# A fused state-space mixer with an MLP gate: four weight loads on another queue, two exponentials on another engine, another order

## The chip, the cores and the metric

The kernel runs on one core of a Trainium2 chip. The core has four compute engines that run side by side, each with its own instruction stream: TensorE (PE in the profile) multiplies matrices into PSUM, VectorE (DVE) and ScalarE (ACT) work on SBUF and PSUM, GpSimd (POOL) works on SBUF. SyncE (SP) issues transfers; ScalarE and GpSimd have queues for transfers too. Engines wait for each other through semaphores. The metric is the time of one execution in microseconds, here the median of several runs.

## The reference, cut to what matters

```python
xn = layernorm(x)                                 # x: 1 x 2048 x 448
dt = exp(log_dt); Lam_bar = exp(dt * Lam)         # Lam complex, 448 states
B_bar = ((Lam_bar - 1) / Lam)[:, None] * Bmat
Bu = einsum("bld,pd->blp", xn, B_bar)
h[t] = Lam_bar * h[t-1] + Bu[t]                   # over 2048 steps
s = 2 * Re(einsum("blp,dp->bld", h, Cmat)) + xn * Dskip
m = gelu(layernorm(xn) @ w1 + b1) @ w2 + b2       # 448 -> 1792 -> 448
out = x + s * silu(m)
```

Inputs and output are bfloat16.

## The kernel before, in words

The 2048 positions are cut into 8 blocks of 256, a block into its even and its odd positions (par 0 and 1), each 128 rows on the partitions. Two blocks make a group of 512 positions; the loop over the four groups is written out by `STEPS`. For each group:

- VectorE takes the statistics (bn_stats, L399; for group 0's first layer norm L431), makes the factors (`ln_scale`), and VectorE or ScalarE apply them (L499, L500). A DMA transpose or TensorE turns the normalized rows into columns.
- `mm1_run` (L801) multiplies by w1. The contraction over 448 goes in halves of 64 rows, two at a time on two halves of TensorE. ScalarE applies GELU out of PSUM (L805). `mm2` (L828) multiplies by w2; VectorE adds the bias (L831); ScalarE makes SiLU (L833) or tanh (L835).
- `bu` (L729) multiplies by the input matrix BT; the result u is copied out of PSUM (`copy`, L417). `ssm` turns u by tables of sines and cosines WT (L744 to L748), scans along the positions with the decay dk (L753, L755), copies the scanned states to bf16 (L417), and turns them back (L771 to L775). L773 and L775 write the state h_sb; L775, called hh below, is the part for the last 64 states.
- `ym` (L871, L877) multiplies the state by CZ (even positions, with M applied to xn, L874) or CQ (odd positions). VectorE multiplies by the gate (L885, L888) and adds x (L891), and the result is written out.

Before that, tables are made: the parameter columns in `parameters` (three vectors of 448 turned into columns by TensorE at L529, then dozens of operations on 128 x 4 at L534 to L566), a range reduction `wrap` and a sine polynomial, the tables WT and dk in `tables`, the matrices CZ, CQ and BT's second half with `combine` (a scaled tmp at L658 or L659, and a multiply-add at L661), and M in `m0`.

Group 0's first two blocks have a start of their own. `first_stats` takes statistics and makes the layer norm factor 1/sqrt(var'). For block 0 ScalarE does it for each parity by Ln and Exp (L434, L435), for block 1 for both parities at once (L438, L439). `first_apply` applies the factor on VectorE (L453), TensorE transposes (L460) and L417 copies the result out of PSUM. `dummies` (L422) are matmuls of ones that fill TensorE's time ahead of the work. ScalarE's function tables have to be loaded: Ln and Exp at the start (L314), GELU in `gelu_table` (L443), Sin and SiLU (L614), GELU again (L618).

w1 lies in SBUF as 128 rows x 4 x 1792. `ldw1` loads it in four pieces of columns; for each piece one transfer brings rows 0 to 383 and a second one the last 64 rows (w1r), both on SyncE's queue; the low half of the last slice is copied on the chip (L352). `ldx` loads x by blocks; the one of blocks 2 and 3 is SyncE's twelfth transfer.

The order of the work is not found at run time. The builder functions only list tasks, each with what it reads and writes. `Plan.emit` then issues them in the order of `ORDER`, a list of task numbers written out by hand; each engine's instruction stream is that list filtered to its tasks. Where a task can run on one of two engines (`small`: GpSimd or VectorE; `copy`: ScalarE or VectorE; `combine`, `ln_apply`, output adds), it goes to the second one if its number stands in `SECOND`. Waits on semaphores are put in from the reads and writes.

## Time and profile before

| what | value |
|---|---|
| median of three runs | 153.37 us (153.15 to 153.41) |
| span of the profiled execution | 151.8 us |
| TensorE busy | 147.1 us, 97% |
| VectorE busy | 127.6 us, 84% |
| ScalarE busy | 99.0 us, 65% |
| GpSimd busy | 42.1 us, 28% |

The span goes from the first to the last instruction of the profiled execution; what a run's time has beside it lies around it. A row of the timeline has the start and the duration in us, the engine, the line of the kernel, the operation, the tiles, and in brackets the idle time ahead of it and what ended that; rows of like instructions are drawn together (x8). In the chain that ended last each piece is a start, a duration and what ran. The groups of instructions have busy time and the mean of one in ns. Matmuls overlap in their pipeline, so the mean duration of one is longer than the step from one start to the next.

```profile
PE   7899999999999999999999999999999999999992
...
DVE  2874999999978979999999996379968726999984
ACT  3888996988789559997898610463579834067400
POOL 5376827153020920010456006200072031000201
PEclk9999999999999999999999999999999999999999
DMA  4999999989997300700003032610331001100022
```

These rows of the page cut the span into 40 slices; a digit is the busy share in tenths.

### The profile page before, as it was taken

The page shows a single profiled execution, that of the slowest core. Times are in us where ns is not written, and L with a number is a line of the kernel's source. Part 1 is how long each engine was busy: PE and PEld are TensorE (multiplying, and loading weights), DVE is VectorE, ACT ScalarE, POOL GpSimd, SP SyncE. Part 2 cuts the span into 40 slices and gives each one's busy share as a digit, 9 for nine tenths or more (in the row PEclk, how much of TensorE's full clock was granted, in tenths as well). Part 3 has the DMA queues.
Part 4 walks back from the last instruction along what each step waited for, and adds up shares of the span by engine and source line. Part 5 has one row for each costly group of instructions (what it writes and reads, how often), then busy time and mean ns, then how long its engine had stood idle before and what let it go on. Part 6 is the DMA issues. An engine that isn't in the chain of part 4 may idle for free.

```text
span 151.8 us, 2974 instructions
## 1 busy us (share of the span) xinstructions
PE 147.1 (97%) x1127; PEld 86.6 (57%) x1127; DVE 127.6 (84%) x267; ACT 99.0 (65%) x183; POOL 42.1 (28%) x101
## 2 busy tenths in 40 slices
PE   7899999999999999999999999999999999999992
PEld 7785755454566577545444556764454666555551
DVE  2874999999978979999999996379968726999984
ACT  3888996988789559997898610463579834067400
POOL 5376827153020920010456006200072031000201
PEclk9999999999999999999999999999999999999999
DMA  4999999989997300700003032610331001100022
GB/s 116 262 305 390 266 202 138 219 152 133 165 261 180 65 0 0 138 0 4 0 0 63 4 60 45 154 60 4 60 101 23 0 4 57 64 0 0 4 84 98
DMA packets 31236, 14.73 MB, mean 97 GB/s; under 512 B 24752, under 2 KB 30774, under 8 KB 31222
## 3 DMA queue, kind: packets, MB, share of 16 engines
q1 hardware_dynamic: 30912, 14.26, 41.8%
q0 software_dynamic: 160, 0.23, 1.0%
q8 instruction: 9, 0.15, 0.4%
q10 hardware_dynamic: 150, 0.05, 0.1%
q14 instruction: 5, 0.04, 0.1%
HBM read 6.89 MB, written 1.84 MB: 57 GB/s over the span
## 4 chain that ended last, share of the span: by engine, by line
PE 80%; DVE 9%; DMA 4%; SPq 4%; issue 2%
PE psum L828 23%; PE psum L801 22%; PE psum L729 14%; PE psum L871 13%; DMA x_all<-in_A_x_dram 4%; PE psum L874 4%; SPq L84 4%; PE psum L712 3%; DVE xn_sb L499 2%; DVE lnst L399 1%; DVE s_w L628 1%; PE psum L877 1%; DVE o L831 1%; PE psum L697 1%; DVE tmp L891 1%
## 5 line engine op out<-in xcount | busy, mean ns | idle before, releaser
L801 PE MATMUL psum<-xn2T,w_sb 64*128 64x512 bf16 (+1 forms) x462 | 44.6, 345 | 0.3 <-ACT xn2T L417 0.2
L828 PE MATMUL psum<-w_sb,gT 128*128 128x448 bf16 x224 | 44.5, 353 | 0.2 <-DVE o L831 0.2
L805 ACT ACTIVATE gT<-psum,b1f 128x512 bf16<-128x512 f32 (+1 forms) x66 | 35.9, 625 | 10.4 <-PE psum L801 10.2
L801 PEld LDWEIGHTS psum<-xn2T,w_sb 64*128 64x128 bf16 x462 | 24.1, 109 | 19.8 <-ACT gT L805 2.3
L828 PEld LDWEIGHTS psum<-w_sb,gT 128*128 128x128 bf16 x224 | 21.5, 98 | 20.7 <-DVE o L831 0.6
L417 ACT ACTIVATE u_sb<-psum 128x512 bf16<-128x512 f32 (+2 forms) x22 | 10.5, 478 | 23.0 <-PE psum L729 22.7
L729 PE MATMUL psum<-xnT,BT 128*128 128x256 bf16 x196 | 24.0, 273 | 0.0
L729 PEld LDWEIGHTS psum<-xnT,BT 128*128 128x128 bf16 x196 | 18.9, 98 | 5.4 <-issue 1.1
L891 POOL TENSOR_TENSOR tmp<-t,x_all 128x448 bf16<-128x448 bf16 x5 | 5.2, 1032 | 33.1 <-DVE t L888 30.7
L753 DVE TENSOR_TENSOR_SCAN s_w<-dk,vs 128x774 f32<-128x774 f32 x8 | 14.0, 1760 | 0.1
L500 ACT ACTIVATE xn_sb<-x_all,lnw 128x448 bf16<-128x448 bf16 (+2 forms) x21 | 13.0, 662 | 1.2 <-DVE xn_sb L499 1.1
L417 ACT ACTIVATE vs<-s_w 64x256 bf16<-64x256 f32 (+2 forms) x16 | 10.9, 681 | 2.6 <-DVE s_w L753 1.5
L871 PE MATMUL psum<-CZ,h_sb 128*128 128x448 bf16 x56 | 11.9, 352 | 0.0
L871 PE MATMUL psum<-CQ,h_sb 128*128 128x448 bf16 (+2 forms) x54 | 10.5, 332 | 0.0
L399 DVE BATCH_NORM_STATS2 lnst<-x_all 128x6 f32<-128x448 bf16 x12 | 7.1, 617 | 3.4 <-DMA x_all<-in_A_x_dram 3.4
L831 DVE TENSOR_TENSOR o<-psum,b2bc 128x448 f32<-128x448 f32 x16 | 9.7, 614 | 0.2
L871 PEld LDWEIGHTS psum<-CZ,h_sb 128*128 128x128 bf16 x56 | 5.4, 98 | 4.7 <-DVE lnmv L405 0.4
L871 PEld LDWEIGHTS psum<-CQ,h_sb 128*128 128x128 bf16 x54 | 5.1, 98 | 4.0 <-DVE t L885 0.4
L874 PE MATMUL psum<-M,xnT 128*128 128x448 bf16 x32 | 7.4, 352 | 0.0
L480 POOL TENSOR_TENSOR lnw<-lnw,mhalf 128x8 f32<-128x8 f32 x3 | 7.2, 2404 | 0.3
L883 DVE TENSOR_TENSOR Cr<-psum,xd 128x448 f32<-128x448 f32 x7 | 4.3, 620 | 3.5 <-PE psum L877 3.4
L499 DVE TENSOR_SCALAR xn_sb<-x_all,lnw 128x448 bf16<-128x448 bf16 (+2 forms) x19 | 6.9, 396 | 0.0
(160 smaller groups left out, 189.1 us busy)
## 6 DMA issues: line engine op xcount, KB each, us to landing
out_dram<-tmp SPq DMA_DIRECT2D x7, 224.0 KB, 2.0
x_all<-in_A_x_dram SPq DMA_DIRECT2D x3, 448.0 KB, 4.0
w_sb<-in_B_w_dram SPq DMA_DIRECT2D x3, 448.0 KB, 8.4
w_sb<-in_B_w_dram SPq DMA_DIRECT2D x3, 384.0 KB, 4.8
vs<-in_A_C_re_dram SPq DMA_DIRECT2D x1, 392.0 KB, 11.6
Bn<-in_A_B_im_dram SPq DMA_DIRECT2D x1, 336.0 KB, 10.2
Bn<-in_A_B_re_dram SPq DMA_DIRECT2D x1, 336.0 KB, 10.5
vs<-in_A_C_im_dram SPq DMA_DIRECT2D x1, 336.0 KB, 10.8
```

The source lines that it names most:

```text
L399: dve([lambda e, b=b, par=par, q=q: e.bn_stats(lnst[:, q, :], x_all[:, 2 * g + b, par, :])], [f"x{2 * g + b}"] , [f"st{q}"], 0.62, prio)
L417: kb.either(("act", [lambda e, o=o, i=i: e.activation(o, i, ACT.Copy) for o, i in pairs]), ("dve", [lambda e, o=o, i=i: e.tensor_copy(o, i ...
L499: on = [("dve", [lambda e, o=o, i=i: e.tensor_scalar(o, i, rs, nb, op0=ALU.mult, op1=ALU.add) for o, i in parts], 0.4, 0.12), ("act", [lam ...
L500: ("act", [lambda e, o=o, i=i: e.activation(o, i, ACT.Identity, bias=nb, scale=rs) for o, i in parts], 0.75, 0.2)]
L729: fns = [lambda e, r=r, m=m, d=d: e.matmul(psum[:, 4, r * NK:(r + 1) * NK], BT[:, m, d, :], xnT[:, gx, d, :], start=(d == 0), stop=(d == 6 ...
L753: dve(lambda e, so=so, vi=vi: e.tensor_tensor_scan(so, dk[:].rearrange("p i c -> p (i c)"), vi, 0.0, ALU.mult, ALU.add), ["v", "vl", "dk", ...
L801: return lambda e: e.matmul(view(bk[k]), w1_sb[rows, d, fcol(2 * j + k)], rhs[rows, d, :, :], start=not second and n == 0, stop=second and ...
L805: act([lambda e, k=k: e.activation(gT[:, gb, 2 * j + k, :].rearrange("p (r c) -> p r c", r=2)[:, :, cols], view(bk[k]), ACT.Gelu_apprx_tan ...
L828: fns = [lambda e, fi=fi: e.matmul(psum[:, bk, 0:D], gT[:, gb, fi, q * 128:(q + 1) * 128], w2_sb[:, fi, :], start=(fi == 0), stop=(fi == N ...
L831: dve(lambda e: e.tensor_tensor(o2[:, fb, :], psum[:, bk, 0:D], b2bc[:], ALU.add), [f"ps{bk}", "b2bc"], [f"oo{fb}"], 0.62, prio - 76)
L871: fns = [lambda e, k=k: e.matmul(psum[:, bk, c0:c1], h_sb[:, hb, k, k0:k0 + 128], cm[:, k, c0:c1], start=(k == 0), stop=False) for k in ra ...
L874: fns += [lambda e, d=d: e.matmul(psum[:, bk, c0:c1], xnT[:, gx, d, xs], M0[:, d, c0:c1], start=False, stop=(d == 3)) for d in range(4)]
```

## The change

Four things change.

1. The four transfers of w1's last 64 rows are issued by ScalarE instead of SyncE.
2. Block 1's two layer norm factors are no longer made by Ln and Exp on ScalarE. A `small` task w11 computes var' (VectorE in the new lists), and GpSimd raises it to the power -1/2 (128 x 2). The decay R1 = exp(A1) is no longer an Exp on ScalarE; GpSimd raises a constant e, set by a new memset, to the power A1 (128 x 4).
3. The task that loads the GELU table reads only dt and block 0's factors, no longer R1 and block 1's factors.
4. `ORDER` and `SECOND` are new throughout. By task numbers, the list has two more tasks (the memset and w11), so numbers from 14 on are shifted by one or two against the old list.

What the new lists say for the start: ScalarE issues Lambda_im, log_dt, w1r of piece 1, Lambda_re, then loads the first table, makes a factor of block 0, issues w1r of piece 0, makes the other factor, and issues w1r of pieces 2 and 3 around its copy of the second transposed half; the first half's copy is VectorE's. SyncE's order is the two halves of x block 0, block 1, w1 pieces 1, 0, 2, 3, then x blocks 2 and 3 as the eighth transfer, then w2. TensorE's eight dummies stand ahead of the parameter matmuls. Further on, fifteen of the parameter operations, the wrap, carries and some output adds go from GpSimd to VectorE; a dozen copies, tmp halves and layer norm applies go from ScalarE to VectorE, and about as many from VectorE to ScalarE, among them the |.| of the tables. The last column of CZ is computed after group 0's state instead of before it.

```diff
 ORDER = [int(k) for k in """
-0 13 19 47 9 16 18 20 14 1 94 26 17 95 91 27 92 21 15 24 48 4 96 12 108 93 90 109 97 104 103 25 105 99 22 98 49 50 55 5 51 65 106 2 110 100 111 107 29
-101 112 30 56 28 52 114 23 54 32 53 131 57 117 128 31 118 113 121 170 115 33 46 132 168 133 129 39 130 34 66 171 253 250 102 119 155 40 123 251 252
...
+48 17 9 20 25 19 18 28 21 2 3 16 12 27 14 13 4 15 0 26 22 95 6 30 1 96 92 97 33 91 23 93 110 47 49 100 94 111 105 50 31 40 106 52 98 5 51 107 41 112
+108 53 113 109 42 54 34 114 99 116 101 43 29 104 171 115 39 102 172 120 103 24 119 38 117 121 67 133 130 206 123 170 118 157 134 32 131 173 124 125
...
+617 622 627 624 631 628 625 629 632 626 633 630 634
 """.split()]
 SECOND = [int(k) for k in """
-45 53 54 61 63 66 69 74 76 83 112 130 133 158 160 162 163 165 177 184 185 187 189 190 220 222 224 226 228 230 238 248 249 258 266 268 331 362 364 365
-384 400 401 436 447 468 480 482 487 491 499 501 502 504 510 528 529 609 612 627
+46 55 59 62 63 64 68 70 71 72 73 74 76 77 78 81 82 83 84 85 86 88 102 109 114 132 135 160 163 164 167 186 189 190 191 196 198 204 222 226 230 232 234
+246 248 250 251 260 270 326 355 356 364 366 399 403 404 405 452 470 482 503 504 506 507 509 510 514 518 527 530 532 533 576 591 614 629
 """.split()]
...
 
         ident = SB("ident", [128, 128])
         mhalf = SB("mhalf", [128, 1, 1], F32)
+        euler = SB("euler", [128, 1], F32)
         dk = SB("dk", [128, 3, NK + 2], F32)
         iota = dk[:, 0, 0:NK]
         sgn = SB("sgn", [128, 4], F32)
...
             pool(lambda e: e.memset(M0[:, 3, :], 0.0), [], ["M0p"], 0.3, S0 + 1)
             pool(lambda e: e.memset(h_sb[:, :, :, 0:2], 0.0), [], ["hp0", "hp1"], 0.2, S0 + 1)
             pool(lambda e: e.memset(mhalf[:], -0.5), [], ["mhalf"], 0.1, S0 + 1)
+            pool(lambda e: e.memset(euler[:], math.e), [], ["euler"])
             pool(lambda e: e.memset(eps[:, 0:1], LN_EPS), [], ["eps"], 0.1, S0)
             pool(lambda e: e.memset(eps[:, 1:2], LN_EPS * LN_EPS), ["eps"], ["eps"], 0.1, S0)
 
...
             def ldw1(cs, prio):
                 a, w = CH[cs[0]][0] * 128, sum(CH[c][1] for c in cs) * 128
                 ld("sp", w1_sb[:, 0:3, a:a + w], dram_ap(B_w1, a, [[F, 128], [128 * F, 3], [1, w]]), [f"w1_{c}" for c in cs], 384 * w * 2, prio, dur=0.55)
-                ld("sp", w1_sb[64:128, 3, a:a + w], dram_ap(B_w1, 384 * F + a, [[F, 64], [1, w]]), [f"w1r_{c}" for c in cs], 64 * w * 2, prio)
+                ld("act", w1_sb[64:128, 3, a:a + w], dram_ap(B_w1, 384 * F + a, [[F, 64], [1, w]]), [f"w1r_{c}" for c in cs], 64 * w * 2, prio)
                 for c in cs:
                     a, w = CH[c][0] * 128, CH[c][1] * 128
                     low, high = w1_sb[0:64, 3, a:a + w], w1_sb[64:128, 2, a:a + w]
...
                         kb.add("act", [lambda e, var=var, r1=r1: e.activation(r1, var, ACT.Ln, scale=1.0 + LN_EPS, bias=eps[:, 1:2]),
                                        lambda e, r1=r1: e.activation(r1, r1, ACT.Exp, scale=-0.5)], [f"mv0_{q}", "eps", "warm"], [f"r1{q}"], chain=True)
                     elif par == 1:
-                        vs2, rs2 = lnmv[:, 0, 1:4:2, 1], lnw[:, 0, 2, 1, 1:4:2]
-                        kb.add("act", [lambda e: e.activation(rs2, vs2, ACT.Ln, scale=1.0 + LN_EPS, bias=eps[:, 1:2]),
-                                       lambda e: e.activation(rs2, rs2, ACT.Exp, scale=-0.5)], ["mv0_1", "mv0_3", "eps", "warm"], ["r11", "r13"], chain=True)
+                        vs2, ws2, rs2 = lnmv[:, 0, 1:4:2, 1], lnw[:, 0, 1, 1, 1:4:2], lnw[:, 0, 2, 1, 1:4:2]
+                        small(lambda e: e.tensor_scalar(ws2, vs2, 1.0 + LN_EPS, LN_EPS * LN_EPS, op0=ALU.mult, op1=ALU.add), ["mv0_1", "mv0_3"], ["w11"])
+                        pool(lambda e: e.tensor_tensor(rs2, ws2, mhalf[:, 0, :].to_broadcast([128, 2]), ALU.pow), ["w11", "mhalf"], ["r11", "r13"])
 
             def gelu_table():
                 kb._sem("gelu0")
-                kb.add("act", lambda e: e.preload_act_table_set("gelu_apprx_tanh_and_others"), ["cr", "r10", "r12"] + ["r11", "r13"] * (not 0), ["Wg0"], sem="gelu0")
+                kb.add("act", lambda e: e.preload_act_table_set("gelu_apprx_tanh_and_others"), ["cdt", "r10", "r12"], ["Wg0"], sem="gelu0")
 
             def first_apply(b):
 
...
                 small(lambda e: e.tensor_scalar(col(F2), ang[:, 0, 0, 0, :], 2.0, None, op0=ALU.mult), ["f1"], ["f2"])
                 small(lambda e: e.tensor_scalar(ang[:, 0, 0, 1, :], ang[:, 0, 0, 0, :], 512.0, None, op0=ALU.mult), ["f1"], ["f3"])
                 small(lambda e: e.tensor_tensor(col(A1), col(DT), col(LRE), ALU.mult), ["cdt", "cp"], ["ca"])
-                act(lambda e: e.activation(col(R1), col(A1), ACT.Exp), ["ca"], ["cr"], 0.2, 3 * PINNED - 1, "exp")
+                pool(lambda e: e.tensor_tensor(col(R1), euler[:].to_broadcast([128, 4]), col(A1), ALU.pow), ["ca", "euler"], ["cr"])
                 wrap = [(lambda e: e.tensor_scalar(YB, YA, ROUND, None, op0=ALU.add)),
                         (lambda e: e.tensor_scalar(YB, YB, ROUND, None, op0=ALU.subtract)),
                         (lambda e: e.tensor_tensor(YA, YA, YB, ALU.subtract))]
```

29 rows, old and new, of the table ORDER are left out of this document.

## The prediction, made before the result was known

> **What bounds the kernel now.** I read the page first, then the chain that ended last, the windows by engine, and the timelines of the places the change touches.
>
> ```profile
> PE 147.1 (97%) x1127; PEld 86.6 (57%) x1127; DVE 127.6 (84%) x267; ACT 99.0 (65%) x183; POOL 42.1 (28%) x101
> ```
>
> ```profile
> 2.67 0.55 SPq L84
> ...
> 6.77 6.79 DMA x_all<-in_A_x_dram
> ...
> 18.64 0.18 DVE lnw L485
> ...
> 18.84 0.23 DVE lnw L486
> ...
> 27.33 2.82 PE psum L828 x14
> ...
> 67.64 9.86 PE psum L801 x89
> ...
> 148.22 0.12 PE psum L877
> ```
>
> ```profile
> 7.00:16.00 9.00, 9.00 (x132) 6.67 (x130) 5.91 (x21) 7.88 (x19) 6.04 (x18) 1.00 1.04 340
> 16.00:27.30 11.30, 11.02 (x90) 6.11 (x86) 10.85 (x38) 9.89 (x19) 6.55 (x21) 1.00 1.15 194
> ...
> 40.00:60.00 20.00, 20.00 (x147) 13.62 (x146) 17.48 (x40) 15.30 (x28) 5.34 (x11) 1.00 0.49 107
> 60.00:80.00 20.00, 20.00 (x153) 10.06 (x152) 19.83 (x39) 17.69 (x35) 4.57 (x8) 1.00 0.14 27
> ```
>
> The last view's columns are stretch and length, then busy time of PE, PEld, DVE, ACT and POOL, the granted clock, the DMA share, GB/s. TensorE runs without a break from 27.33 to 148.34; no matmul is removed. So the end moves only by what happens before TensorE becomes dense, or by a new hole. The candidate for a new hole is VectorE: 19.83 of 20 us busy at 60 to 80, still 2.52 idle at 40 to 60, and before that it follows the landing of x blocks 2 and 3 (issue 6.77, landed 13.56).
>
> **The start.** Part one moves four 64-row loads from SyncE's queue to ScalarE's.
>
> ```profile
> 1.61 0.27 ACTq L84 DMA_DIRECT2D dk<-in_A_Lambda_re_dram  x1
> 4.03 0.21 PE L529 MATMUL psum<-ident,dk 3*128 3x3 bf16 x3 [0.27 <-DMA dk<-in_A_Lambda_re_dram]
> 4.32 0.87 PE L422 MATMUL psum<-const-bfloat16-1.0 128*128 128x128 bf16 x8
> 5.03 0.38 PE L460 MATMUL psum<-ident,xn_sb 128*128 128x128 bf16 x4
> 5.25 0.34 PE L422 MATMUL psum<-const-bfloat16-1.0 128*128 128x128 bf16 x3
> 5.45 1.25 ACT L417 ACTIVATE xn2T<-psum 128x512 bf16<-128x512 bf16 x2
> 6.60 0.29 ACT L438 ACTIVATE lnw<-lnmv,eps 128x2 f32<-128x2 f32 x1
> 6.85 2.50 PE L801 MATMUL psum<-xn2T,w_sb 64*128 64x256 bf16 x42 [0.19 <-ACT xn2T L417]
> 6.92 0.20 ACT L439 ACTIVATE lnw<-lnw 128x2 f32<-128x2 f32 x1
> 7.03 0.19 ACT L541 ACTIVATE cw<-cw 128x4 f32<-128x4 f32 x1
> 7.29 1.28 ACT L443 ACT_TABLE_LOAD   x1
> 8.67 2.30 ACT L805 ACTIVATE gT<-psum,b1f 128x256 bf16<-128x256 f32 x6
> ```
>
> On ScalarE the third issue is now a w1 load, ahead of Lambda_re: at SyncE's 0.55 it pushes Lambda_re's issue from 1.61 to 2.16, so what waits at 4.03 starts at about 4.6; the eight dummies now stand before the parameter matmuls, so the first transposes move from 5.03 to about 5.5. The remaining three issues, 0.55 each, stand between block 0's two factors, ahead of the second evacuation, and after it. On the other side the two evacuations of 1.25 together no longer follow each other: VectorE takes one. I get the second evacuation's end at 7.0 instead of 6.7, and the first mm1 matmul at 7.15: **+0.3**. Bounds: −0.45 if the issues cost ScalarE nothing (only the parallel evacuation counts), +0.6 if all the lateness of the transposes passes on.
>
> Part two takes 0.29 + 0.20 and 0.19 from ScalarE and lets the GELU table wait only for dt and block 0's factors. Naming 0.68 as the gain would be wrong: in ScalarE's order the fourth w1 issue (0.55) now stands before the table load and its second evacuation is late. The table goes from 7.29 to about 7.05, the first GELU from 8.67 to 8.5; mm1 itself starts 0.3 later, so the first results can't be used much sooner. I enter 0. If the queue did not hold it, the bound is −0.4.
>
> The power's price:
>
> ```profile
> L480 POOL TENSOR_TENSOR lnw<-lnw,mhalf x3: 1897/2261/3053, 9.3 to 78.2; 128x8 f32<-128x8 f32 x3
> ```
>
> Eight columns took 1.90 to 3.05. Two columns lie between the 0.19 of a four-column ACTIVATE (L541), as if power were nothing special, and 1.90; if the price goes by columns it is 1.90 × 2/8 = 0.48, and I take 0.6. Block 1's transposes are due near 9.35, when the 42 matmuls from 6.85 end. Their factors' work starts at 6.60 today; with 0.16 for w11 and 0.6 for the power they would be ready at about 7.4, hardly later than today's 7.12: covered by those matmuls, **0**. At 1.90 they come at 8.7, two applies of 0.39 and ScalarE's or VectorE's evacuation follow, and TensorE waits about 0.9. The four-column power of the decay, at 0.95, stands after the sine chain and is needed only by VectorE's tables after 20: 0, up to +0.4 as lateness of the parameters.
>
> **x blocks 2 and 3.**
>
> ```profile
> 13.58 2.21 DVE L399 BATCH_NORM_STATS2 lnst<-x_all 128x6 f32<-128x448 bf16 x4 [1.95 <-DMA x_all<-in_A_x_dram]
> ```
>
> SyncE's issue of them moves from twelfth to eighth: four issues at 0.55 less, 2.2 earlier. But the DMA share is 1.04 at 7 to 16 and the bytes ahead of it are the same, so the landing is set by the engines: 13.55 becomes 13.2, **−0.35** for VectorE (bounds 0 and −2.2). [...]
>
> **The other order** is the largest part. I counted what VectorE does up to the last product of group 1's state (hh1, L775), which TensorE's ym of group 1 (L871) waits for.
>
> ```profile
> L831 DVE TENSOR_TENSOR o<-psum,b2bc 128x448 f32<-128x448 f32 x16 | 9.7, 614 | 0.2
> ...
> L891 DVE TENSOR_TENSOR tmp<-t,x_all 128x448 bf16<-128x448 bf16 x10 | 3.8, 386 | 0.1
> ...
> L659 DVE TENSOR_SCALAR tmp<-Cr,cw 128x448 f32<-128x448 bf16 x7 | 3.1, 452 | 0.3 <-POOL cw L561 0.2
> ...
> L499 DVE TENSOR_SCALAR xn_sb<-x_all,lnw 128x448 bf16<-128x448 bf16 x7 | 2.7, 387 | 0.0
> ...
> L417 DVE CAST u_sb<-psum 128x512 bf16<-128x512 f32 x2 | 1.4, 684 | 0.1
> ...
> L631 DVE SCALAR_TENSOR_TENSOR s_w<-s_w 128x1024 f32<-128x1024 f32 x1 | 1.2, 1226 | 0.0
> ...
> L626 DVE TENSOR_SCALAR s_w<-s_w 128x1024 f32<-128x1024 f32 x1 | 0.7, 694 | 0.0
> ...
> L561 DVE TENSOR_TENSOR cw<-cw 128x4 f32<-128x4 f32 x4 | 0.6, 156 | 0.0
> ```
>
> ```profile
> 67.31 0.61 DVE L399 BATCH_NORM_STATS2 lnst<-x_all 128x6 f32<-128x448 bf16 x1
> 67.85 0.66 DVE L661 SCALAR_TENSOR_TENSOR CZ<-Cr,cw,tmp 128x448 bf16<-128x448 bf16 x1
> ...
> 90.62 0.28 DVE L775 TENSOR_TENSOR h_sb<-pa 128x256 bf16<-128x256 bf16 x1
> ```
>
> ```profile
> 77.44 1.49 PE L871 MATMUL psum<-CZ,h_sb 128*128 128x448 bf16 x7
> ...
> 92.28 1.49 PE L871 MATMUL psum<-CZ,h_sb 128*128 128x448 bf16 x7
> ```
>
> Added to VectorE before that point: 25 small operations (parameters, wrap, w11, carry) × 0.156 = 3.9; six scaled tmp halves or wholes × 0.45 = 2.7; one evacuation and three LN applies, four × 0.39 = 1.6; the group 0 evacuation u0 0.68; the first copy of the scanned states to bf16, which no row shows on VectorE: 1.04 by L626 × 1.5, 2.05 by three of the 0.684, I take 1.04; one diagonal product 0.2; an output add 0.39; two o/xr operations that now come sooner 1.23. Sum 11.7. Taken away: the |.| of the tables 1.23; seven tmp parts 3.2; M's copy about 0.6 and u1, both by the 0.684; a skip product 0.39; three LN applies 1.2; six small 0.9; two that now come later 1.0. Sum 9.2. That leaves +2.5; consecutive starts overlap by 0.07 (67.31 + 0.61 against 67.85), dependent small ones step by 0.20 instead of 0.156, for some 18 instructions more: −1.3 and +0.9 are the extremes, I take **+2.3**.
>
> The state ends at 90.90 now and TensorE wants it at 92.28: slack 1.38. So 2.3 − 0.35 − 1.38 = +0.57. VectorE itself waits for TensorE's and ScalarE's products, which I walked forward in the new order: the wait of the |angle| for VectorE's wrap, behind four statistics of 0.61, holds GELUs near 16 (0.3 of hole, about paid back by mm2 matmuls pulled in between); the second GELU table about 0.45 later; group 2's mm1 at about 68.1 instead of 67.64. So VectorE's own work begins about 0.5 later: **+1.1 in all at 93.4**. One place sooner, the last CZ column moves behind group 0's state and much of group 1's input: it ended at 68.51 with 8.9 to spare before 77.44, now near 78.6; its hole of 0.5 or 0.6 lies inside the 1.1, not beside it. Group 2's u1 goes to VectorE (0.68, behind other work): **+0.3**. After it I find no later hole; the output adds that move from POOL to VectorE cost it 0.386 each, after the state that TensorE waits for.
>
> Sum: 2.3 − 0.35 − 1.38 + 0.55 + 0.3 = **+1.4**. The start's +0.3 is swallowed by the later hole. The profiled span is 151.8, the median of the runs 153.37: 1.57 lie around the span and stay. 151.8 + 1.4 + 1.57 = **154.8**.
>
> **Rivals.** *Faster*: the queue did matter. x blocks 2 and 3 land 2.2 earlier (11.35), the VectorE excess is paid in advance (2.3 − 2.2 − 1.38 < 0), no hole comes, and the parallel evacuation starts mm1 0.45 sooner; with the 0.28 of TensorE idle at 16 to 27.3 that gives −0.7: 152.7. For it: VectorE's 1.95 of idle time ahead of L399 waits for this transfer alone. Against: the DMA share of 1.04. It decides once the landing comes before 12.5 or so: 0.27. *No change*: the excess goes into VectorE's 2.52 idle at 40 to 60 and the start's lateness into the waits before 27.33: 153.4, 0.13. *Power at full price*: 1.90 for two columns, TensorE waits 0.9 near 9.5, and since all behind it shifts too, 154.8 + 0.6 = 155.4: 0.10. *The clock*:
>
> ```profile
> 0.83 2.93 PE L422 MATMUL psum<-const-bfloat16-1.0 128*128 128x128 bf16 x26 [0.83 <-PEq L1006]
> ```
>
> The dummies start every 0.105 in this row (26 in 2.93, the last 0.31 long), and every 0.06 in the row of three at 5.25; TensorE's pause ahead of 4.03 grows from 0.27 to 0.8. If this delays the faster pace by some 3 us, mm1 runs at half pace for about 1.2 us: +0.6, 155.4: 0.07.
>
> [...]
>
> **Numbers.** The forecast itself has 0.43, with its own range 153.8 to 156.0. Faster by over 0.2% (0.3 us, what a measurement can tell here) 0.27, within 0.13, slower 0.60. The range goes from the faster rival to a state copy of 2.05 with the small operations at 0.20 (+1.9): 152.6 to 156.7.
>
> **What would show it.** Right: first mm1 at 7.0 to 7.3; x blocks 2 and 3 land after 12.8; TensorE idle in front of group 1's first ym near 93, released by VectorE's L775 line. Wrong: that idle is absent, or TensorE becomes dense and stays so from an earlier time; a two-column power above 1.5; or a hole elsewhere, at the mm1 near 9.5 or the last 30 us.

## The result, and the profile after

| what | before | after |
|---|---|---|
| median of four runs | 153.39 us (153.15 to 153.68) | 157.87 us (156.53, 157.96, 158.08, 157.78) |
| ratio, 95% interval | 1 | 1.0279 (1.0238 to 1.032) |
| span of the profiled execution | 151.8 us | 154.5 us (time of this execution 156.53) |

The changed kernel is slower by 4.5 us; the prediction had 154.8 with a range up to 156.7, so the direction was right and the time lies above the range. The profiled execution is the fastest of the four, 1.3 under the median, so its trace can account for 2.7 us of span and not for all of the 4.5; two more traces of the same kernel, taken later, show another 2.0 and 2.9 us of span (last experiment). An execution more than 1.5% above the fastest one of its kernel is called slow and is left out of the medians and ratios below; the traces of e4, e5 and e6 are of such executions.

The page's first part, and its row of TensorE in 40 slices, after:

```profile
PE 147.1 (95%) x1127; PEld 87.0 (56%) x1127; DVE 132.2 (86%) x297; ACT 95.0 (61%) x178; POOL 29.1 (19%) x77
...
PE   7659999999999999999999999999999999999992
```

TensorE does the same 147.1 us of work. What is new is idle time, and it stands in the second and third slice (3.9 to 11.6 us), not in the middle where the prediction looked for it: slices four to 39 are full. The timeline of TensorE after, at these two slices (start, duration, in brackets the idle time ahead and what ended it):

```profile
5.02 0.64 PE L424 MATMUL psum<-const-bfloat16-1.0 128*128 128x128 bf16 x8 [1.25 <-DMA dk<-in_A_Lambda_re_dram]
...
7.26 0.27 PE L604 MATMUL psum<-ident,dk 4*128 4x3 bf16 x4 [0.38 <-DMA dk<-in_B_b_dram]
...
7.51 0.52 PE L803 MATMUL psum<-xn2T,w_sb 64*128 64x256 bf16 x6
9.78 2.14 PE L803 MATMUL psum<-xn2T,w_sb 64*128 64x256 bf16 x36 [1.75 <-DMA w_sb<-in_B_w_dram]
```

Three waits for transfers, one behind the other. The third is the large one: six mm1 matmuls run, and then TensorE stands for 1.75 us until a piece of w1 has landed. The chain that ended last, after, says which:

```profile
2.17 0.45 ACTq L84
2.65 1.29 ACT L315
...
4.30 5.35 DMA w_sb<-in_B_w_dram
```

This is the second transfer (the 64 rows, called the rest below) of w1's piece 0. On ScalarE's stream it stands behind Lambda_re's issue, the table load and one of block 0's factors, is issued at 4.30 and lands 5.35 later. Before, it was SyncE's: the views of DMA issues, of before around 3.88 and of after around 4.30 and 4.52 (KB each, last the time from issue to landing):

```profile
w_sb<-in_B_w_dram SPq DMA_DIRECT2D x1, 32.0 KB, 3.1
```

```profile
x_all<-in_A_x_dram SPq DMA_DIRECT2D x1, 448.0 KB, 6.6
w_sb<-in_B_w_dram ACTq DMA_DIRECT2D x1, 32.0 KB, 5.3
```

Issued 0.42 later it lands 2.6 later, at 9.64 instead of 7.01. In the meantime SyncE has issued all four main pieces (its timeline after: four from 2.19 to 4.47), and 32 KB now stand behind most of their bytes.

```profile
2.19 2.28 SPq L84 DMA_DIRECT2D w_sb<-in_B_w_dram  x4
4.52 0.49 SPq L84 DMA_DIRECT2D x_all<-in_A_x_dram  x1
```

The view of the DMA queues after shows it. Most of SyncE's transfers are q1 there, ScalarE's are q10. From 5 to 7.9 us q1 takes the time of all 16 DMA engines, and q10 doesn't appear; from 8 to 9.7 it does (packets, MB, share of the engines' time):

```profile
q1 hardware_dynamic: 1119, 0.91, 100.5%
```

```profile
q1 hardware_dynamic: 453, 0.59, 97.0%
q10 hardware_dynamic: 78, 0.03, 8.1%
```

The rest lands beside the last main piece, which SyncE issues at 3.98 and which lands at 9.81.

The new order makes it worse in one more way: the matmuls that need piece 0 are the second group of mm1 (from the seventh matmul on), where before they were the fourth.

How late TensorE is, at the same amount of work done, is worked out from the start of each matmul in the two traces (the columns streamed before it, the ones matmuls left out). Lateness against the profiled execution of before:

| before's time | 7.07 | 7.43 | 17.1 | 28.3 | 38.7 | 44.2 | 64.3 | 90.0 | 148.7 |
|---|---|---|---|---|---|---|---|---|---|
| after | +0.69 | +2.59 | +2.75 | +1.90 | +1.85 | +2.30 | +2.68 | +2.85 | +2.77 |

The loss is made by 7.5 us of before's time (10 us after). Between 17 and 28 us the new order gains 0.9, behind 39 us it gives that back, and it adds nothing.

The hole that the prediction expected near 93 is not there. VectorE's and TensorE's timelines after:

```profile
94.68 0.28 DVE L777 TENSOR_TENSOR h_sb<-pa 128x256 bf16<-128x256 bf16 x1
```

```profile
93.60 1.69 PE L731 MATMUL psum<-xnT,BT 128*128 128x256 bf16 x14
95.13 1.49 PE L873 MATMUL psum<-CZ,h_sb 128*128 128x448 bf16 x7
```

The state is ready at 94.96 and wanted at 95.13. The slack of 1.38 is used up but for 0.17, and TensorE doesn't wait.

### The profile page after: what moved, and what is told of

It reads as the page before. It is cut to its first block, busy times and chain, and to the rows that moved or that the text cites. A ratio compares the mean times of both kernels' runs of the same rounds, so it can differ in the third digit from the quotient of the medians.

```text
span 154.5 us, 2961 instructions
## 1 busy us (share of the span) xinstructions
PE 147.1 (95%) x1127; PEld 87.0 (56%) x1127; DVE 132.2 (86%) x297; ACT 95.0 (61%) x178; POOL 29.1 (19%) x77
## 4 chain that ended last, share of the span: by engine, by line
PE 91%; DMA 3%; ACTq 1%; ACT 1%; DVE 1%; issue 1%
PE psum L803 28%; PE psum L830 28%; PE psum L731 14%; PE psum L873 13%; PE psum L876 4%; DMA w_sb<-in_B_w_dram 3%; PE psum L714 3%; ACTq L84 1%; PE psum L879 1%; ACT L315 1%; PE psum L699 1%; DVE tmp L893 1%; PE psum L462 0%; DVE t L887 0%; ACT lnw L436 0%
## 5 line engine op out<-in xcount | busy, mean ns | idle before, releaser
L807 ACT ACTIVATE gT<-psum,b1f 128x512 bf16<-128x512 f32 (+1 forms) x66 | 36.4, 623 | 13.5 <-PE psum L803 13.2
L803 PEld LDWEIGHTS psum<-xn2T,w_sb 64*128 64x128 bf16 x462 | 24.8, 109 | 21.1 <-issue 3.7
L419 ACT ACTIVATE u_sb<-psum 128x512 bf16<-128x512 f32 (+2 forms) x18 | 8.7, 485 | 14.7 <-PE psum L731 14.7
L419 ACT ACTIVATE vs<-s_w 64x256 bf16<-64x256 f32 (+2 forms) x14 | 7.9, 566 | 4.2 <-DVE s_w L757 2.5
L837 ACT ACTIVATE th<-o 128x448 f32<-128x448 f32 x8 | 4.7, 582 | 4.0 <-DVE o L833 4.0
L893 DVE TENSOR_TENSOR tmp<-t,x_all 128x448 bf16<-128x448 bf16 x15 | 6.6, 442 | 0.1
L838 DVE SCALAR_TENSOR_TENSOR g_sb<-th,o 128x448 bf16<-128x448 f32 x8 | 4.9, 615 | 1.9 <-ACT th L837 1.9
L893 POOL TENSOR_TENSOR tmp<-t,Cr 128x256 bf16<-128x256 bf16 x1 | 0.8, 750 | 30.7 <-DVE t L887 30.7
## 6 DMA issues: line engine op xcount, KB each, us to landing
vs<-in_A_C_re_dram SPq DMA_DIRECT2D x1, 392.0 KB, 11.6
Bn<-in_A_B_re_dram SPq DMA_DIRECT2D x1, 336.0 KB, 11.6
```

Source lines behind the costliest of these rows:

```text
L419: kb.either(("act", [lambda e, o=o, i=i: e.activation(o, i, ACT.Copy) for o, i in pairs]), ("dve", [lambda e, o=o, i=i: e.tensor_copy(o, i ...
L803: return lambda e: e.matmul(view(bk[k]), w1_sb[rows, d, fcol(2 * j + k)], rhs[rows, d, :, :], start=not second and n == 0, stop=second and ...
L807: act([lambda e, k=k: e.activation(gT[:, gb, 2 * j + k, :].rearrange("p (r c) -> p r c", r=2)[:, :, cols], view(bk[k]), ACT.Gelu_apprx_tan ...
L893: add = lambda e: e.tensor_tensor(o_sb[:, ob, par * D + c0:par * D + c1], t3[:, fb, c0:c1], res, ALU.add)
```

## The experiments

Theory A: the rest of w1 is late, by the time at which it is issued, whatever the queue. Theory D: a pause of TensorE in the start costs it the full pace for some microseconds afterwards. The rivals are: transfers on ScalarE's queue are slow as such (theory B in the expectations), the order's added work on VectorE (C), the order of GpSimd's first tasks (E), and the powers; F is about one move on TensorE. Measured beside the experiments, the kernel before took 153.4 to 153.6 in the median. Tasks are named by their numbers in the new list: 27, 22, 30, 33 are w1's main pieces 1, 0, 2, 3, each followed in number by its rest (28, 23, 31, 34); 16 is Lambda_re, 4 the first table, 25 and 26 the two loads of b1 on GpSimd, 0 and 1 the two parts of ident.

### Undo the queue: e1_all_sp, and the queue alone: e4_queue_old_order

The changed kernel, with each rest on SyncE right behind its main piece:

```diff
-                ld("act", w1_sb[64:128, 3, a:a + w], dram_ap(B_w1, 384 * F + a, [[F, 64], [1, w]]), [f"w1r_{c}" for c in cs], 64 * w * 2, prio)
+                ld("sp", w1_sb[64:128, 3, a:a + w], dram_ap(B_w1, 384 * F + a, [[F, 64], [1, w]]), [f"w1r_{c}" for c in cs], 64 * w * 2, prio)
-48 17 9 20 25 19 18 28 21 2 3 16 12 27 14 13 4 15 0 26 22 95 6 30 1 96 92 97 33 91 23 93
+48 17 9 20 25 19 18 21 2 3 16 12 27 28 14 13 4 15 0 26 22 23 95 6 30 31 1 96 92 97 33 34
...
```

> The changed kernel with all four w1 rest loads back on SyncE's queue, each right behind its main load; everything else as changed. Theory A (the 1.75 us hole in front of 9.78 is piece 0's rest load, which ScalarE issues at 4.30 when SyncE has already queued pieces 1, 0, 2 and 3): the hole goes, first mm1 at about 7.2, blocks 2 and 3 of x land near 13.3 again, and the time falls from 157.9 by 2 us or more, to 154.5 to 156.0. Theory C (the new order itself costs most of the 4.5 us, further on): the hole goes but VectorE's lateness opens a new one near 93, and the time stays above 156.5.

The kernel before, with the four rests on ScalarE and nothing else:

```diff
-                ld("sp", w1_sb[64:128, 3, a:a + w], dram_ap(B_w1, 384 * F + a, [[F, 64], [1, w]]), [f"w1r_{c}" for c in cs], 64 * w * 2, prio)
+                ld("act", w1_sb[64:128, 3, a:a + w], dram_ap(B_w1, 384 * F + a, [[F, 64], [1, w]]), [f"w1r_{c}" for c in cs], 64 * w * 2, prio)
```

> The kernel before, in its old order, with only the four rest loads on ScalarE's queue at the places where the old list has them (piece 0's behind both factors of block 0, near 5.1). Theory A: piece 0's rest lands after 9, TensorE waits about 2 us in front of mm1, time 155.0 to 156.0 against 153.4. Theory C: the queue is harmless in an order that is not the new one, time within 0.5 of 153.4.

Undone: 154.47 us (12 runs), ratio 1.0085 (1.0052 to 1.0118). Alone: 157.7 (4 runs), ratio 1.0281 (1.0235 to 1.0327). Moving the four transfers costs 3.4 us in the new order (157.87 − 154.47) and 4.3 in the old one, and the rest of the change about 1.05. Between the two profiled executions, of the changed kernel and of e1, the span differs by 1.9 (154.5 − 152.6), and in both mm1 runs near full pace (36 matmuls in 2.14 us after, 42 in 2.93 in e1); by that, about 1.9 of the 3.4 is late data, and the other 1.5 is left for the pace (an estimate from one trace each). TensorE's timeline in e1 and in e4; the profiled execution of e4 is its longest (160.27), so its rows tell the kind of loss and not its usual size:

```profile
7.07 2.93 PE L803 MATMUL psum<-xn2T,w_sb 64*128 64x256 bf16 x42
```

```profile
5.16 0.21 PE L529 MATMUL psum<-ident,dk 3*128 3x3 bf16 x3 [1.40 <-DMA dk<-in_A_Lambda_re_dram]
...
8.43 2.33 PE L801 MATMUL psum<-xn2T,w_sb 64*128 64x256 bf16 x20 [0.28 <-ACT xn2T L417]
12.73 1.68 PE L801 MATMUL psum<-xn2T,w_sb 64*128 64x256 bf16 x14 [1.97 <-DMA w_sb<-in_B_w_dram]
```

In e1 all 42 matmuls run through. In e4 the same two waits as after appear in the old order, and 20 matmuls take 2.33 us, 0.117 each against 0.060 before (42 in 2.50 us): this is theory D, taken up below.

### The powers alone: e7_powers_old_order

The kernel before with parts 2 and 3 of the change in the old order; the new memset stands behind mhalf's, w11 and the power where Ln and Exp stood.

```diff
-                        kb.add("act", [lambda e: e.activation(rs2, vs2, ACT.Ln, scale=1.0 + LN_EPS, bias=eps[:, 1:2]),
-                                       lambda e: e.activation(rs2, rs2, ACT.Exp, scale=-0.5)], ["mv0_1", "mv0_3", "eps", "warm"], ["r11", "r13"], chain=True)
+                        small(lambda e: e.tensor_scalar(ws2, vs2, 1.0 + LN_EPS, LN_EPS * LN_EPS, op0=ALU.mult, op1=ALU.add), ["mv0_1", "mv0_3"], ["w11"])
+                        pool(lambda e: e.tensor_tensor(rs2, ws2, mhalf[:, 0, :].to_broadcast([128, 2]), ALU.pow), ["w11", "mhalf"], ["r11", "r13"])
...
-                act(lambda e: e.activation(col(R1), col(A1), ACT.Exp), ["ca"], ["cr"], 0.2, 3 * PINNED - 1, "exp")
+                pool(lambda e: e.tensor_tensor(col(R1), euler[:].to_broadcast([128, 4]), col(A1), ALU.pow), ["ca", "euler"], ["cr"])
```

> The kernel before with parts two and three alone: w11 on VectorE, both powers on GpSimd, the GELU table freed; rest loads on SyncE and the old order, the new operations at the places of the ones that they replace. If parts two and three cost nothing, as the prediction has it: 153.4 within 0.3, power 128x2 near 0.76. If GpSimd's serial work in front of the layer norm is their price: 153.9 to 154.6, with TensorE waiting ahead of block 1's transposes.

153.34 us, ratio 0.9996 (0.9968 to 1.0024). The powers and the freer table cost nothing and bring nothing that this measurement can tell. Their price, in the groups of the two lines after (min/median/max in ns, first and last start):

```profile
L441 POOL TENSOR_TENSOR lnw<-lnw,mhalf x1: 757/757/757, 8.8 to 8.8; 128x2 f32<-128x2 f32 x1
```

```profile
L543 POOL TENSOR_TENSOR cw<-euler,cw x1: 1171/1171/1171, 22.4 to 22.4; 128x4 f32<-128x4 f32 x1
```

### Only piece 0 mended: e2_piece0_sp, e3_piece0_early

In e2 the rest of piece 0 alone goes back to SyncE; in e3 it stays on ScalarE, ahead of the table.

```diff
-                ld("act", w1_sb[64:128, 3, a:a + w], dram_ap(B_w1, 384 * F + a, [[F, 64], [1, w]]), [f"w1r_{c}" for c in cs], 64 * w * 2, prio)
+                ld("sp" if cs[0] == 0 else "act", w1_sb[64:128, 3, a:a + w], dram_ap(B_w1, 384 * F + a, [[F, 64], [1, w]]), [f"w1r_{c}" for c in cs], 64 * w * 2, prio)
-48 17 9 20 25 19 18 28 21 2 3 16 12 27 14 13 4 15 0 26 22 95
+48 17 9 20 25 19 18 28 21 2 3 16 12 27 14 13 4 15 0 26 22 23 95
...
```

> The changed kernel with only piece 0's rest load on SyncE's queue, behind piece 0's main load; the other three stay on ScalarE's. Theory A: this one transfer is the hole; it lands before 7.6, the hole goes, time 154.8 to 156.3; blocks 2 and 3 of x still land near 11.5, and as VectorE has them sooner the time is not above that of the kernel with all four on SyncE. Theory B (transfers on ScalarE's queue are served slowly as such): pieces 2 and 3 still land at 12 to 13.5 and mm1 waits for one of them near 11, so half of the hole stays, time 156.5 to 157.2.

```diff
-48 17 9 20 25 19 18 28 21 2 3 16 12 27 14 13 4
+48 17 9 20 25 19 18 28 21 2 3 16 23 12 27 14 13 4
...
```

> The changed kernel with piece 0's rest load still on ScalarE's queue but issued right behind Lambda_re and ahead of the table load, near 2.65 instead of 4.30. Theory A: issued before SyncE's backlog it lands by 7.0, the hole is gone, time 155 to 156.5. Theory B: the queue is slow as such, it lands after 8 (5.3 us behind its issue), a hole of at least 0.5 us stays, time 156.5 to 157.5.

e2: 156.4 us, ratio 1.0176 (1.0125 to 1.0227). e3: 156.61, 1.0199 (1.0158 to 1.024). Both are a little above what was expected. In e3 the rest of piece 0 stays on ScalarE's queue, is issued at 2.67, and by the view of DMA issues lands 4.1 later, at 6.75, earlier than before (7.01):

```profile
w_sb<-in_B_w_dram ACTq DMA_DIRECT2D x1, 32.0 KB, 4.1
```

So the queue as such (theory B) doesn't make the hole; the time of the issue does. The hole is gone in both runs, yet only a third of the loss comes back. The groups of TensorE's instructions early in mm1 tell why, before (7 to 9 us) and e2 (7 to 9.6 us, with mm1 from 7.38); the second number behind the bar is the mean duration of one in ns:

```profile
L801 PE MATMUL psum<-xn2T,w_sb 64*128 64x256 bf16 x40 | 2.4, 270 | 0.2 <-ACT xn2T L417 0.2
```

```profile
L803 PE MATMUL psum<-xn2T,w_sb 64*128 64x256 bf16 x22 | 2.5, 414 | 0.1
```

40 matmuls in about 2 us in the one case, 22 in 2.2 us in the other, without a wait between them. A matmul starts every 0.107 us on average instead of every 0.055. The windows of e2, with the granted clock third from the end, show that TensorE had the full pace behind its first pause and lost it again:

```profile
5.00:6.80 1.80, 1.75 (x26) 1.43 (x26) 1.58 (x4) 0.55 (x4) 0.54 (x2) 1.00 1.11 356
7.00:10.00 3.00, 2.94 (x32) 2.51 (x34) 2.28 (x12) 1.65 (x3) 1.20 (x4) 0.50 1.02 348
10.40:14.00 3.60, 3.39 (x51) 2.53 (x49) 2.68 (x8) 2.54 (x7) 3.27 (x8) 1.00 1.04 378
```

In e3 the half pace shows itself in another way: the matmuls start every 0.107 us from the first of the kernel until 11.6, and the column stays at 1.00. The trace's clock records explain the difference: they begin with the first change to the full clock, at 11.6 in e3, and the view counts the time without a record as 1.00. So there are two ways of losing time: the full pace comes late, which the column doesn't show, or it comes and is taken back, which the column shows as 0.50.

### A pause alone: e9_before_pause

The kernel before with fewer ones matmuls, so that TensorE stands still ahead of the parameter matmuls as it does after the change. No transfer is moved.

```diff
-            dummies(26)
+            dummies(12)
```

> The kernel before with nothing changed but the first dummies, 12 instead of 26: TensorE pauses for about 1.7 us before the parameter matmuls (2.3 to 4.0); all real work has the same inputs at the same time. Theory D (a pause of a microsecond or more ahead of mm1 costs some 3 us of half pace): mm1 steps of 0.107 instead of 0.055 for part of 7 to 11, time 154.5 to 156.5 in most runs. If only the waits count and the pace doesn't: 153.4, since no real work starts later.

154.55 us (12 runs), ratio 1.0063 (1.0025 to 1.01): **1.2 us for a pause that delays no work of its own**. TensorE's timeline and its mm1 group between 7 and 9 us in this run:

```profile
3.42 0.21 PE L529 MATMUL psum<-ident,dk 3*128 3x3 bf16 x3 [1.15 <-DMA dk<-in_A_Lambda_re_dram]
...
7.05 3.15 PE L801 MATMUL psum<-xn2T,w_sb 64*128 64x256 bf16 x42 [0.28 <-ACT xn2T L417]
```

```profile
L801 PE MATMUL psum<-xn2T,w_sb 64*128 64x256 bf16 x24 | 2.2, 346 | 0.3 <-ACT xn2T L417 0.3
```

42 matmuls take 3.15 us against 2.50 before. Here the full pace comes late: the step is 0.107 from the first matmul on and becomes 0.055 at 8.5 us; before, it does at 4.9. The profiled execution is the shortest of twelve (153.99), so the 0.65 in it is the lower end; of a longer one there is no trace in this run. Theory D holds in this form: fewer ones matmuls and a pause of 1.15 us put off the full pace, and that alone costs time.

### Bridge the pause: e6_bridge, e8_piece0_sp_bridge

40 ones matmuls instead of 26, in the changed kernel (e6) and in e2 (e8).

```diff
-            dummies(26)
+            dummies(40)
```

> The changed kernel with 14 more of the first dummies (40 instead of 26), which fill TensorE's pause between 3.76 and 5.0; the hole in front of piece 0 stays. Theory D (the pause costs the full pace in most runs: 157.9 is a half-paced start, 156.5 a full-paced one): all runs near 156.4, within 0.5 of each other, mm1 steps of 0.055 from the first on. If the pace has nothing to do with it: 157.9 as before.

> The changed kernel with piece 0's rest load on SyncE (no hole, 156.4 with mm1 at half pace until 10.2) and 14 more dummies over the pause. Theory D: mm1 at full pace throughout, time 154.6 to 155.2, near the 154.5 of the kernel with all four on SyncE. Otherwise 156.4 again.

e6: 156.82 us (5 runs), ratio 1.0221 (1.0178 to 1.0265); the first pause is closed, the wait for the rest of piece 0 stays (1.4), and behind it the granted clock is 0.50 from 10.2 to 13.6. e8: 156.6 (4 runs), 1.0211 (1.0181 to 1.024); its trace has a granted clock of 1.000 over the span, but TensorE waits 0.6 for b1, and from start to start it stands still by 0.9 ahead of 11.79, at matmuls that need the rest of piece 2. Both missed: filling TensorE's first pause brings little while later waits stay, and in e6's trace the pace is lost behind one of them.

### Mend ScalarE's stream: e5_lambda_first, e11_act_mended, e13_three_mended

All four rests on ScalarE, Lambda_re and the rests of pieces 1 and 0 ahead of the table (e5); the same with GpSimd's start of before, ident first and b1's second load right behind the first (e11); piece 0 on SyncE by the edit of e2, the other three on ScalarE, with Lambda_re ahead of them and GpSimd's start (e13).

```diff
-48 17 9 20 25 19 18 28 21 2 3 16 12 27 14 13 4 15 0 26 22 95
+48 17 9 20 25 19 18 16 28 23 21 2 3 12 27 14 13 4 15 0 26 22 95
...
```

> The changed kernel with another order on ScalarE's queue alone: Lambda_re third as in the kernel before, then the rest loads of pieces 1 and 0, then the table load; all four rest loads stay on ScalarE. Theory A+D (the loss is where the rest loads stand on ScalarE's queue: one pushes Lambda_re, so that TensorE pauses for 1.25 us instead of 0.27 and its pace falls to half in most runs; piece 0 comes late): the pause closes to about 0.3, no hole, first mm1 near 7.2 at full pace, time 154.3 to 155.3. Theory B (ScalarE's queue as such): pieces 1, 2 or 3 are late in front of mm1 and the time stays above 156.

```diff
-48 17 9 20 25 19 18 28 21 2 3 16 12 27 14 13 4 15 0 26 22 95
+48 17 9 20 0 1 25 26 19 18 16 28 23 21 2 3 12 27 14 13 4 15 22 95
...
```

> The changed kernel with all four rest loads on ScalarE, but Lambda_re ahead of them, piece 0's ahead of the table load, and GpSimd's start as before. Theory A+E (ScalarE's queue costs by what it is put ahead of and by late issues, not as such): no wait on w1 or b1 in TensorE's list of waits, fast runs at 154.0 to 154.8. Theory B (as such): TensorE still waits for a piece, or the whole start slides because all transfers share the engines; above 155.

```diff
-48 17 9 20 25 19 18 28 21 2 3 16 12 27 14 13 4 15 0 26 22 95
+48 17 9 20 0 1 25 26 19 18 16 28 21 2 3 12 27 14 13 4 15 22 23 95
...
```

> The changed kernel with piece 0's rest load on SyncE, Lambda_re ahead of piece 1's rest load on ScalarE, and GpSimd's start as before; pieces 1, 2 and 3 stay on ScalarE. Theory A+D+E (three faults, not the queue as such): no pause, no hole, full pace from the first mm1 matmul on, x blocks 2 and 3 landed near 11.5, time 153.7 to 154.3, the same as with all four on SyncE and GpSimd's start mended (153.9). Theory B (the queue as such): above 155.

155.54 (3 runs; ratio 1.0144, 1.0122 to 1.0166), 155.82 (1.0144, 1.0104 to 1.0184) and 155.6 (1.0127, 1.0076 to 1.0177): better than the changed kernel, and all three above their expectation. For e11 and e13 the times are those that theory B foretold (above 155); e3 speaks against its mechanism, a queue that is slow as such, and the traces show others. In e5 and e11 two more issues ahead of the table than before make block 0's factor late, and the transposes wait for VectorE's apply (1.0 us in two waits in each trace). Then mm1 runs at half pace: the granted clock is 0.50 from 7.7 to 11.1 in e11 and from 7.2 to 14.0 in e5. TensorE's timeline of e11:

```profile
5.49 0.40 PE L462 MATMUL psum<-ident,xn_sb 128*128 128x128 bf16 x4 [0.69 <-DVE xn_sb L455]
...
7.33 4.15 PE L803 MATMUL psum<-xn2T,w_sb 64*128 64x256 bf16 x42 [0.21 <-DVE b1f L607]
```

In e13 the pace is near full (42 mm1 matmuls in 2.67 us from 6.94), but the rests of pieces 2 and 3 are late as that of piece 0 was; its timeline of TensorE, and its issues between 5.11 and 5.8:

```profile
10.77 1.30 PE L803 MATMUL psum<-xn2T,w_sb 64*128 64x256 bf16 x20 [0.60 <-issue]
12.26 2.11 PE L803 MATMUL psum<-xn2T,w_sb 64*128 64x512 bf16 x21 [0.19 <-issue]
```

```profile
w_sb<-in_B_w_dram ACTq DMA_DIRECT2D x2, 64.0 KB, 6.0
```

The profile names "issue" for these waits, but the steps from start to start stand still by 0.77 and 0.41 right where the rests of pieces 2 and 3 land (10.67 and 12.17). So no place on ScalarE's stream was found that is early enough for the rests and leaves the factors on time.

### What is left of the order: e10, e12, e14, e15

e10 is e1 with GpSimd's start of before; the diff is against e1.

```diff
-48 17 9 20 25 19 18 21 2 3 16 12 27 28 14 13 4 15 0 26 22 23 95 6 30 31 1 96
+48 17 9 20 0 1 25 26 19 18 21 2 3 16 12 27 28 14 13 4 15 22 23 95 6 30 31 96
...
```

> The changed kernel with the four rest loads on SyncE (154.47) and GpSimd's start as before: ident first, both b1 loads right behind it. Theory E (0.4 to 0.6 of the 1.05 that this kernel still loses stands in the start: the b1 columns wait for their second load until 6.8 and ident comes at 4.3): first mm1 at or below 6.9, time 153.8 to 154.1. If the order's loss is all behind 40 us: 154.5.

153.9 us (12 runs), ratio 1.0034 (1.0012 to 1.0055). So GpSimd's start, which issues b1's second load at 3.06 instead of 2.33, is 0.57 of the order's 1.05. TensorE's lateness in e10 by the same reckoning: −0.09 at 7.4, −0.67 at 38.7, −0.22 at 44.2, +0.34 at 90, +0.27 at the end. The order does win 0.67 us and loses 0.9 again behind 39. With no late start in the way, this run is also the place to measure the prediction's VectorE term; VectorE's and TensorE's timelines of e10, and VectorE's busy time and instructions from the start to the state, before and in e10:

```profile
92.18 0.28 DVE L777 TENSOR_TENSOR h_sb<-pa 128x256 bf16<-128x256 bf16 x1
```

```profile
92.62 1.49 PE L873 MATMUL psum<-CZ,h_sb 128*128 128x448 bf16 x7
```

```profile
0.00:90.90 90.90, 80.72 (x192) 1.00 0.61 130
```

```profile
0.00:92.46 92.46, 82.11 (x210) 1.00 0.57 128
```

The state is ready at 92.46, 1.56 later than before (90.90); TensorE comes 0.34 later; 0.16 of the slack is left. The 1.56 is VectorE's own work: 18 instructions more and 1.39 us more busy time. Its idle time up to the state is nearly the same, 10.18 before and 10.35 in e10, so the added work is not hidden in waits.

e12 gives e7 the new order's earlier first six matmuls of mm2 (task 273, diff against e7); e14 is e10 with the first u evacuated by ScalarE again (326 out of SECOND); e15 is e14 with six tmp products back on their old engines.

```diff
-163 141 149 147 148 177
+163 141 149 147 273 148 177
...
-175 179 273 274 275
+175 179 274 275
```

> The old order with the powers (153.34) and one thing taken from the new order: the first six matmuls of mm2 stand three mm1 phases earlier on TensorE, where before it waits 0.28 twice for GELUs (17.4 and 18.5). Theory F (the new order's gain of 0.5 near 17 to 20 comes from this one move): 152.7 to 153.0, faster than both kernels. Otherwise 153.3, the wait only moves.

```diff
-246 248 250 251 260 270 326 355 356
+246 248 250 251 260 270 355 356
```

> The changed kernel with all four on SyncE and GpSimd's start mended (153.9), and u0 copied out of PSUM by ScalarE as before instead of VectorE. If u0 on VectorE, behind other work there, is the 0.4 us wait in front of the second bu at 42.5: 153.5 to 153.6. If the wait comes with the GELU that is late at 41.3, it stays: 153.9.

```diff
-186 189 190 191 196 198 204 222 226 230
+186 189 190 191 192 222 224 226 228 230
```

> As the run with u0 on ScalarE, and six tmp products between 28 and 41 us on the engines that had them before (four of them leave ScalarE, where they stand between GELUs). If they make the GELU late at 41.3 (0.33): 153.0 to 153.3, not above the kernel before. If VectorE becomes late instead: 153.6 or more.

e12: 154.63 us, 1.0083 (1.0044 to 1.0122); a miss, since TensorE's waits in this run have a new one at 28.6, and nothing is gained:

```profile
PE psum L830 <- DVE o L833: 0.9, 1, 0.9
```

e14: 153.97, 1.0034 (0.9999 to 1.007), the same as e10. e15: 154.74, 1.0094 (1.0054 to 1.0134), worse. Neither single edit explains the 0.9 that the order gives back behind 39; that stays open, and so does what wins its 0.67. By the reckoning of lateness it is won between 17 and 28 us, and e7, in the old order, wins 0.34 there too (+0.18 to −0.16), so not all of it need be the order's. No version made here is faster than before.

### The changed kernel again: e16_after_again, e17_after_third

No edit; the question was why the median is 1.3 above the profiled execution.

> The changed kernel as it is, for the trace of another execution. Three of its four executions took 157.8 to 158.1, the profiled one 156.5. Theory A+D (late rest of w1 piece 0, and TensorE at half pace behind a pause): an execution near 158 shows the same landing of piece 0's rest (9.5 to 9.8) and the same hole of 1.6 to 1.9, and in addition mm1 matmuls at a step of about 0.107 for some 1.3 us more than in the profiled execution, in front of the hole or behind it. Rival: a longer hole (landing after 10.5), with the pace as in the first profile.

> The changed kernel once more, one look, in case the first look falls near 156.5. Same expectations.

e16: 159.35 profiled (span 157.4), 159.03 once more; e17: 158.48 (span 156.5). TensorE's timelines of e16 and e17:

```profile
4.95 1.03 PE L424 MATMUL psum<-const-bfloat16-1.0 128*128 128x128 bf16 x8 [1.19 <-DMA dk<-in_A_Lambda_re_dram]
...
10.28 4.02 PE L803 MATMUL psum<-xn2T,w_sb 64*128 64x256 bf16 x36 [1.13 <-DMA w_sb<-in_B_w_dram]
```

```profile
4.32 1.03 PE L424 MATMUL psum<-const-bfloat16-1.0 128*128 128x128 bf16 x8 [0.56 <-DMA dk<-in_A_Lambda_re_dram]
...
10.34 3.71 PE L803 MATMUL psum<-xn2T,w_sb 64*128 64x256 bf16 x36 [1.58 <-DMA w_sb<-in_B_w_dram]
```

Put them beside the rows of after: the eight ones matmuls take 1.03 instead of 0.64, and the 36 mm1 matmuls behind the hole 4.02 and 3.71 instead of 2.14. The pieces of e16's 2.9 us (157.4 − 154.5) can be read off: the hole ends 0.5 later, 1.9 on the 36 matmuls, 0.3 on the transposes behind them, 0.3 on the next six. From 16 us on the two traces run parallel to the end. So these two executions of the changed kernel have the same hole (1.13 and 1.58) and, around it, TensorE at half pace until 15.8 us in e16 and 13.6 in e17; the execution profiled first had the full pace from 5.02 on. In both the full pace comes late, as in e3 and e9. That is theory D, and the rival (a longer hole at the same pace) falls: the rest lands at 10.15 and 10.2, half a microsecond later than in the first trace and a little later than expected. The three executions of 157.8 to 158.1 have no trace. That they lost the pace too is likely but not shown; one of them has a granted clock of 0.978 over its span, as e5 has, whose clock was 0.50 for 6.8 us.

The length of the pause does not decide it alone: like pauses (1.25 in the first trace, 1.19 in e16) had opposite outcomes, and in e16 the dense work from 10.28 gets the step of 0.055 only 5.5 us later, at 15.8. What decides it, these traces do not show. Between the first trace and e16 the pace alone makes about 2.5 of 154.5 us (1.9 + 0.3 + 0.3), 1.6%.

## Why the prediction was right or wrong, point by point

**The start, "+0.3": this is the step that failed.** It counted the four transfers by what their issues cost ScalarE ("the remaining three issues, 0.55 each"), and took for granted that the data come when they came before. No term and no rival asked when the rest of a piece is issued, when it lands and which matmul wants it. Measured: the first mm1 matmul at 7.51 instead of 7.15, then the seventh waits 1.75 for the rest of piece 0, lateness +2.6, and none of it is swallowed by the end (+2.77). e1 and e4 show that the loss comes with these four transfers: 3.4 us undone, 4.3 alone. e3 shows that the late issue makes the hole, not ScalarE's queue as such.

**The clock, "+0.6" with a chance of 0.07.** A full pace that comes late was named and is there (from 8.5 us on in e9, 15.8 in e16, 13.6 in e17, against 4.9 before). No run shows the "some 3 us" of delay that the +0.6 is made from: e9 has the full pace 3.6 later than before, e16 10.9 later, and the trace of after has it right behind its pause (at 5.02). Both the chance and the size were too small: the pause was read as 0.8 and was 1.25, a second and a third wait followed it, and the half pace costs from 0.65 (e9's profiled execution) to about 2.5 us (e16: 1.9 + 0.3 + 0.3) instead of 0.6. The prediction had the full pace delayed, as in e3, e9, e16 and e17; that it can come and be taken back for 3.4 us, as in e2, e6 and e11, or for 6.8, as in e5, it did not have.

**Powers and GELU's table, 0: right.** e7 gives 0.9996. The sizes were near: 0.757 us for two columns against 0.6 taken, 1.171 for four against 0.95 (0.767 and 1.007 in e7). "Power at full price" (1.90) falls.

**x blocks 2 and 3, "−0.35".** The two traces first compared show a landing at 11.11 instead of 13.55, and by the prediction's own words the faster rival would have been decided by that ("before 12.5 or so"). More traces take it back:

| x blocks 2 and 3 | traces | issue | landing |
|---|---|---|---|
| as SyncE's twelfth transfer | before, e1, e7, e9, e10, e12, e14, e15 | 6.76 to 6.78 | 12.0 to 13.6, median 12.3 |
| as SyncE's eighth | after, e3, e4, e5, e6, e11, e16, e17 | 4.48 to 4.67 | 11.0 to 12.8, median 11.8 |
| as its ninth (one rest ahead) | e2, e8, e13 | 5.10 to 5.20 | 10.8 to 11.4 |

Each landing is the issue and the time to landing in the trace. 2.2 us of earlier issue moved the median landing by 0.5, with a spread of over 1.5 us in each of the first two rows. In the three traces of the last row it comes 1.3 earlier than in the first, for 1.6 of earlier issue. So the size is open, between the prediction's −0.35 and about −1.3; the full 2.2 never arrived. More important, the term had no effect to pass on: in e7, with the old order, the transfer landed at 12.2, and both sides of the state's slack stand where they stood (90.74 and 92.12, each 0.16 earlier, as all of TensorE is in that run). VectorE's timeline of e7:

```profile
90.46 0.28 DVE L777 TENSOR_TENSOR h_sb<-pa 128x256 bf16<-128x256 bf16 x1
```

The faster rival falls with it: nine of the eleven early traces land before 12.5 us, and no version is faster than before. The prediction's reason for a small term, a DMA share of 1.04 at 7 to 16 us and the same bytes ahead, fits the first two rows better than the first pair of traces did: most of the 2.2 us is lost. The other direction the prediction left out: the rest of piece 0, issued behind four main pieces, lands with the last of them (9.64 against 9.81); issued behind one, in e3, it lands at 6.75.

**The other order, "+1.1 in all at 93.4".** The direction was right: VectorE's state of group 1 comes 1.56 later in e10. By the prediction's terms it would have been 2.3 − 0.35 + 0.55 = 2.5. It is mis-sized by 0.9, and since the slack is 1.38 and TensorE is itself 0.34 late there, 0.16 remains and no hole opens. The instructions were counted well: some 18 more, and 18 there are, and their durations do add up to 2.5 more (92.2 before, 94.7 in e10). What they cost was not: the +2.3 is +1.39 of busy time, since consecutive instructions overlap. The prediction named that overlap as its lower extreme (−1.3, so +1.2) and then went almost to the full sum. The +0.55 for a later begin of VectorE's work is 0.17 of idle time. One price that no row had shown was taken at 1.04: the copy of 128x1536 from f32 to bf16, which takes 1.216 in the trace after (line 419, twice). So that term was 0.18 too low, in the other direction. The hole near 78 for the last CZ column doesn't come either (lateness after is +2.84 at 75 and +2.85 at 90). The "+0.3" for group 2's u1 does not show: lateness in e10 doesn't grow behind 90.

**The sum.** +1.4 was made of a hole that does not open (+1.1 and +0.3), while the loss that came stood in a step entered at +0.3 and said to be swallowed. That the sign was right is luck; it owes nothing to the working. Of the signs set out beforehand, the two that came were "a hole elsewhere, at the mm1 near 9.5" and the absent idle time near 93. One reading was a little off, and nothing hangs on it: 148.34 is where the chain leaves TensorE, whose last matmul starts at 148.66.

## What to carry to other kernels

When a load is moved to another engine's queue, write down for each transfer three times: when the new stream reaches its issue, which bytes of all queues have been issued before that, and when its first reader wants it; the issue's cost on the engine is the small part. A stream with table loads and dependent operations is a poor place for loads that are wanted within the next 5 us while the DMA engines have several microseconds of backlog: here the rest of piece 0 took 5.35 us from issue to landing, against 3.1 before. And read TensorE's pace from the step between equal matmuls in the first 15 us, not from the granted clock alone: in these runs waits of 1.1 to 1.6 us there cost another 0.65 (e9) to about 2.5 us (e16) around them, in some executions and not in others.
